# A 2048-step FFT convolution inside a GLU block: 28-channel spectrum steps, no exchanged filter loads, half of the second inverse turn through HBM

## The chip, the core and the metric

The kernel runs on one core of one Trainium2 chip. The metric is the device time of one execution in microseconds (us). Engines are named as in the profile: PE (matrix multiplier; PEld is its weight load), DVE (vector engine), ACT (scalar engine), POOL (GpSimd), SP (the queue that issues nearly all DMAs).

## The reference, cut to what matters

```python
x = A_q                                              # [1, 2048, 448], S = 2048, D = 448
sa, ca, ga, sb, cb, gb = split6(silu(c) @ w_mod)     # six rows of 448
h = layernorm(x) * (1 + ca) + sa
kv = causal_conv4(A_k, shift_k) * A_v                # four taps per channel
y = irfft(rfft(kv, 4096) * rfft(ssm_k, 4096))[:2048] + kv * ssm_D   # per channel
x = x + ga * (h * y)
h = layernorm(x) * (1 + cb) + sb
x = x + gb * ((sigmoid(h @ w_gate) * (h @ w_up)) @ w_down)          # 448 -> 1792 -> 448
```

## The kernel before

All of it is float32; the last part splits its operands in two fp32r pieces and multiplies three times.

**Convolution.** The long convolution is a product of spectra. A spectrum is made in three moves. Stage 1 is a matmul (`stage1_k` for the filter, `stage1_v` for the signal). Then `turn(a, i)` swaps, with one DVE instruction, the 32 partitions of each block with the 32 rows, for 28 channels: eight turns (`i` = 0 to 7) do the 224 channels of one half `h` of the model's 448. Stage 2 is a second matmul. The signal's two halves lie in `av[0]` and `av[1]`, the filter's in `ak[0]` and `ak[1]`; each is a tile of 128 partitions x 32 rows x 224 channels. The filter's second half takes its turn through HBM (`turn_out`, `turn_in`, tile `kd`), so `stage2_k(1, n)` can run only when those loads have landed.

**The loop `stage2_v`.** It has 16 steps, p = 8h + n. Step p takes a block of one eighth of `av[h]` (`block`): eight of the 32 rows and 112 of the 224 channels, so the first four blocks need turns 0 to 3 and the last four need turns 4 to 7. A step is: matmuls `s2v` into PSUM, two DVE products `m` with the filter's block (L306 for h = 0, L304 for h = 1), and, one step later, `stage2_back`: matmuls `sa` (L319) and an ACT copy back into `av[h]` (L320). For h = 0 the `s2v` matmuls are made twice, the second time with the real and imaginary rows exchanged. For h = 1 they are made once, and instead the filter's block is loaded once more with its partition groups exchanged: `load_kx`, four DMAs for each step into `kx`.

After every step `beside(h, n)` runs what is placed beside that step by a table on p: further turns, `stage2_k(1, .)`, the sums of the modulation (`mod_load`, `mod_parts`, `mod_sum`), the first layer norm (`ln1_stats` on ACT, `ln1_end` on DVE), and `gates`, which prepares the gate tiles `G` (on POOL; a part on ACT for the second half).

**The inverse.** The spectra take a turn back before the last matmul `stage_out` (tiles `y`). For `av[0]`, channels 0 to 111 go through HBM (`half_out`, `half_in`, scratch `kd0`) and channels 112 to 223 take four DVE turns. For `av[1]` all eight turns are DVE's: p = 13, 14, 15 and five after the loop. `gate` multiplies `y` by `G` and adds to `x1`: on POOL for h = 0, on DVE for h = 1.

**The tail and the GLU.** Between loop and GLU stand the last modulation sums, the first weights' split in two pieces (`split_hi` on ACT, `split_lo` on DVE, L501), `gate(1, 0)`, the second norm (`ln2_stats`, `ln2_end`), `norm_rows` and its transposes (`xn`, `pt`, L732). Then come 56 blocks of gate-and-up matmuls (`gu`, L760) and the down matmuls (`d`, L783), until the end.

Instructions stand in the order of the code (`tc.manual_schedule()`); each engine takes its own in that order and waits on semaphores. The PSUM tiles are `t` (two buffers), `sa` and `y` (one each).

Of the kernel before, what the change touches and what calls it, by code (L numbers as in the profile page):

```python
# [79 lines left out]
def adaln_conv_glu_kernel(ctx: ExitStack, tc: tile.TileContext, q, kT, v, ssm, shift, dskip,  # L80
# [201 lines left out]
    cols4 = lambda t: t.rearrange("p b (j c) -> p b j c", c=DT)  # L282

    def stage2_v(between):


        for h in range(2):
            for n in range(8):
                x, k = block(av[h], n), block(ak[h], n)
                if h:  # L290
                    kx = kxs.pop(n)
                    pt = two("t", f"s2v{h}_{n}")
                    stage2(pt, x)
                else:
                    pts = [two("t", f"s2v{h}_{n}_{b}") for b in range(2)]
                    for ex in range(2):
                        for b in range(2):
                            for r in (0, 64):
                                c = r ^ 64 * b
                                PE.matmul(pts[b][c:c + 64, ex, :D], w2[r:r + 64, ex], x[r:r + 64, b], start=True, stop=True)  # L300
                m = [pairs(quad("m", 4, f"m{h}_{n}_{b}")) for b in range(2)]
                for b in range(2):
                    if h:
                        DVE.tensor_mul(cols4(m[b]), cols4(rows(pt)), kx if b else k)  # L304
                    else:
                        DVE.tensor_mul(cols4(m[b]), cols4(rows(pts[b])), k[:, b].unsqueeze(1).to_broadcast([P, 2, 4, DT]))  # L306
# [4 lines left out]
        stage2_back()

    def stage2_back():
        h, n, m = products.pop(0)
        pt = two("sa", f"sa{h}_{n}")
        for b in range(2):
            for ex in range(2):
                r = slice(64 * ex, 64 * ex + 64)
                PE.matmul(pt[r, b, :D], wa[:, b, r], m[ex][:, b] if h else m[b][:, ex], start=True, stop=True)  # L319
        ACT.activation(block(av[h], n), cols4(rows(pt)), AF.Copy)  # L320

    kxs = {}

    def load_kx(n):

        kx = quad("kx", 2, f"kx{n}").rearrange("p a c -> p (a c)").rearrange("p (b j c) -> p b j c", b=2, c=DT)
        x = block(ak[1], n)
        for r in range(0, P, 32):
            nc.sync.dma_start(kx[r:r + 32], x[r ^ 32:(r ^ 32) + 32])
        kxs[n] = kx  # L330
# [314 lines left out]
    raw = lambda i: late["tmp"][:, NG * C + 512 * i:NG * C + 512 * (i + 1)]

    def beside(h, n):

# [15 lines left out]
        if p in (4, 5) or 8 <= p < 14:  # L664
            load_kx(p - 4 if p < 6 else p - 6)
        if 7 <= p < 11:
            half_in(av[0], kd0, half, p - 7)
        if p in (2, 5, 8, 9):
            ln1_end({2: 0, 5: 1, 8: 2, 9: 3}[p])
        if p in (2, 5) or 8 <= p < 14:  # L670
            next(gating)
        if p in (0, 1, 3, 4, 6, 7):
            ln1_stats({0: 2, 1: 3, 3: 4, 4: 5, 6: 6, 7: 7}[p])
# [2 lines left out]
        if p in (9, 10):
            turn(av[0], 2 * p - 14)
            turn(av[0], 2 * p - 13)
        if p >= 13:
            turn(av[1], p - 13)  # L680
        if p in (12, 13):
            for k in range(3):
                load_raw(0, 3 * (p - 12) + k, raw(3 * (p - 12) + k))
        if p >= 13:
            gate(0, p - 13, y_copy(0, p - 13, stage_out(0, p - 13, "y")), POOL)
# [6 lines left out]
    gate(0, 3, y_copy(0, 3, stage_out(0, 3, "y")), POOL)
    for m in (3, 5):
        mod_parts(m, "sa")
        mod_sum(m)
    rb_.close()
# [232 lines left out]
```

## Time and profile before

| | |
|---|---|
| median of 3 runs | 617.83 us (617.62 to 618.08) |
| the profiled execution's own time | 617.9 us |
| its span, first to last instruction | 616.1 us |
| PE busy | 573.5 us (93% of the span) |
| DVE, ACT, POOL busy | 330.6, 245.3, 80.2 us |
| mean granted PE clock | 0.982 |

A busy share of the whole span says little here: up to about 225 us the work is spread over all engines, after it PE runs almost without a gap. Times below are in us from the span's start.

### The profile page before, as it was taken

The page shows a single profiled execution, that of the slowest core. Times are in us where ns is not written, and L with a number is a line of the kernel's source. Part 1 is how long each engine was busy: PE and PEld are TensorE (multiplying, and loading weights), DVE is VectorE, ACT ScalarE, POOL GpSimd, SP SyncE. Part 2 cuts the span into 40 slices and gives each one's busy share as a digit, 9 for nine tenths or more (in the row PEclk, how much of TensorE's full clock was granted, in tenths as well). Part 3 has the DMA queues.
Part 4 walks back from the last instruction along what each step waited for, and adds up shares of the span by engine and source line. Part 5 has one row for each costly group of instructions (what it writes and reads, how often), then busy time and mean ns, then how long its engine had stood idle before and what let it go on. Part 6 is the DMA issues. An engine that isn't in the chain of part 4 may idle for free.

```text
span 616.1 us, 7497 instructions
## 1 busy us (share of the span) xinstructions
PE 573.5 (93%) x3020; PEld 435.5 (71%) x3020; DVE 330.6 (54%) x409; ACT 245.3 (40%) x429; POOL 80.2 (13%) x69
## 2 busy tenths in 40 slices
PE   7997598979769999999999999999999999999995
PEld 6554222324357788888888888888888888888884
DVE  0999888897987874433443333333334434433332
ACT  5998675776346675511222221222122112211110
POOL 2000004499930000000100000000010001000000
PEclk9999989999879999999999999999999999999999
DMA  8996899688521100000111110111011101000112
GB/s 295 273 324 243 265 214 287 148 163 188 139 66 50 35 1 1 0 1 0 31 51 33 35 41 10 30 35 34 1 30 35 36 0 31 0 1 26 65 60 90
DMA packets 36919, 51.88 MB, mean 84 GB/s; under 512 B 18834, under 2 KB 25748, under 8 KB 36756
## 3 DMA queue, kind: packets, MB, share of 16 engines
q1 hardware_dynamic: 36820, 51.39, 30.2%
q8 instruction: 24, 0.39, 0.3%
q14 instruction: 11, 0.09, 0.0%
q0 software_dynamic: 64, 0.01, 0.0%
HBM read 38.55 MB, written 9.18 MB: 77 GB/s over the span
## 4 chain that ended last, share of the span: by engine, by line
PE 69%; DVE 12%; ACT 7%; DMA 6%; issue 3%; SPq 1%; DVEq 0%; ACTq 0%
PE gu L760 40%; PE d L783 20%; DVE av L175 3%; DMA v<-in_v_dram 2%; PE sa L319 2%; DMA wm<-in_wmod_dram 2%; PE s2v L300 1%; PE pt L732 1%; DMA kT<-in_kT_dram 1%; DVE acc L227 1%; DVE m L306 1%; DMA ssm<-in_ssm_dram 1%; ACT xn L720 1%; DVE st L417 1%; DVE x L786 1%
## 5 line engine op out<-in xcount | busy, mean ns | idle before, releaser
L760 PE MATMUL gu<-xt,wt 128*128 128x512 f32 x1232 | 291.0, 391 | 1.2 <-DVE sg L765 1.2
L760 PEld LDWEIGHTS gu<-xt,wt 128*128 128x128 f32 x1232 | 230.9, 188 | 47.9 <-DVE sg L765 1.7
L765 DVE TENSOR_TENSOR sg<-sg,gu 128x512 f32<-128x512 f32 x56 | 38.4, 686 | 185.4 <-ACT sg L764 185.2
L783 PE MATMUL d<-wt,hh 128*128 128x448 f32 x448 | 127.7, 366 | 3.0 <-DVE x L786 2.7
L764 ACT ACTIVATE sg<-gu 128x512 f32<-128x512 f32 x56 | 33.4, 597 | 236.5 <-PE gu L760 236.5
L783 PEld LDWEIGHTS d<-wt,hh 128*128 128x128 f32 x448 | 83.9, 188 | 13.2 <-issue 1.9
L783 PE MATMUL d<-wt,hl 128*128 128x448 f32 x224 | 81.8, 365 | 0.0
L786 DVE TENSOR_TENSOR x<-x,d 128x896 f32<-128x896 f32 (+1 forms) x57 | 60.7, 1066 | 5.6 <-PE d L783 5.6
L769 DVE TENSOR_TENSOR hl<-sg,hh 128x512 fp32r<-128x512 f32 x56 | 39.2, 700 | 39.2 <-ACT hh L768 39.2
L768 ACT ACTIVATE hh<-sg 128x512 fp32r<-128x512 f32 x56 | 35.4, 633 | 45.6 <-DVE sg L765 45.6
L486 POOL TENSOR_TENSOR r<-r,gbrow 128x448 f32<-128x448 f32 x10 | 11.5, 1157 | 313.4 <-DMA r<-in_wd_dram 307.3
L175 DVE STREAM_TRANSPOSE av<-av 128x896 f32<-128x896 f32 x28 | 50.2, 1841 | 0.0
L783 PEld LDWEIGHTS d<-wt,hl 128*128 128x128 f32 x224 | 42.1, 188 | 3.3
L319 PE MATMUL sa<-m,wa 128*64 128x448 f32 x128 | 30.3, 552 | 5.4 <-DVE m L304 2.1
L319 PEld LDWEIGHTS sa<-m,wa 128*64 128x64 f32 x128 | 8.4, 136 | 26.0 <-issue 14.3
L300 PE MATMUL s2v<-av,w 64*64 64x448 f32 x128 | 17.6, 599 | 5.8 <-DVE av L175 5.6
L320 ACT ACTIVATE av<-sa 128x896 f32<-128x896 f32 x16 | 14.6, 913 | 18.8 <-PE sa L319 18.8
L455 POOL TENSOR_SCALAR G<-x,rstd,nmr 128x224 f32<-128x224 f32 x16 | 8.3, 530 | 96.3 <-DMA wm<-in_wmod_dram 83.5
L306 DVE TENSOR_TENSOR m<-s2v,ak 128x896 f32<-128x896 f32 x16 | 16.6, 1079 | 5.8 <-PE s2v L300 5.7
L501 DVE TENSOR_TENSOR wt<-r,wt 128x512 fp32r<-128x512 f32 (+1 forms) x30 | 19.7, 663 | 0.0
L175 DVE STREAM_TRANSPOSE ak<-ak 128x896 f32<-128x896 f32 x8 | 13.9, 1825 | 8.8 <-ACT ak L199 8.8
L495 ACT ACTIVATE wt<-r 128x512 fp32r<-128x512 f32 (+1 forms) x30 | 17.7, 597 | 0.0
(112 smaller groups left out, 515.8 us busy)
## 6 DMA issues: line engine op xcount, KB each, us to landing
wm<-in_wmod_dram SPq DMA_DIRECT2D x10, 392.0 KB, 5.2
kd<-ak SPq DMA_DIRECT2D x4, 896.0 KB, 8.4
x<-in_q_dram SPq DMA_DIRECT2D x4, 896.0 KB, 11.8
ak<-kd SPq DMA_DIRECT2D x4, 896.0 KB, 15.8
kx<-ak SPq DMA_DIRECT2D x32, 112.0 KB, 3.8
out_dram<-x SPq DMA_DIRECT2D x7, 448.0 KB, 2.5
v<-in_v_dram SPq DMA_DIRECT2D x6, 448.0 KB, 9.8
r<-in_wg_dram SPq DMA_DIRECT2D x10, 256.0 KB, 2.7
```

The lines of the kernel that those rows point to most:

```text
L175: DVE.transpose(x, x)
L300: PE.matmul(pts[b][c:c + 64, ex, :D], w2[r:r + 64, ex], x[r:r + 64, b], start=True, stop=True)
L306: DVE.tensor_mul(cols4(m[b]), cols4(rows(pts[b])), k[:, b].unsqueeze(1).to_broadcast([P, 2, 4, DT]))
L319: PE.matmul(pt[r, b, :D], wa[:, b, r], m[ex][:, b] if h else m[b][:, ex], start=True, stop=True)
L501: DVE.tensor_sub(lo, r, hi)
L760: PE.matmul(pgu[:, s], wts[j][s][k % 2][:, t, f * P:(f + 1) * P], x[:, xs], start=first, stop=not left)
L764: ACT.activation(sg, pgu[:, 0], AF.Sigmoid)
L765: DVE.tensor_mul(sg, sg, pgu[:, 1])
L768: ACT.activation(hh, sg, AF.Copy)
L769: DVE.tensor_sub(hl, sg, hh)
L783: PE.matmul(pt[:, i, :D], h[:, (2 * e + i) * P:(2 * e + i + 1) * P], w[:, f], start=m == 0, stop=m == len(ops) - 1)
L786: DVE.tensor_add(y, y, rows(pt)[:, a:b])
```

## The change

**Blocks.** For h = 0, and for the last four blocks of h = 1, a block is now all 32 rows of the 28 channels of one turn. The first four blocks of h = 1 (`eights`) keep eight rows, and the first 112 channels. Both halves now make the `s2v` matmuls twice, so `load_kx` and its 32 DMAs are gone.

**Stage 1.** The last four groups of `stage1_v` (12 to 15) become `stage1_v_half`: two groups at a time, `av[0]` first, `av[1]` after it, copied by ACT alone; `mod_parts(0)` stands between.

**Turns.** Two turns stand ahead of the loop where there were five; a table `TURNS` places the others. Channels 0 to 111 of `av[1]` come back through HBM: `eight_out` after steps 9 to 12, `half_in` after step 13. Four inverse turns of `av[1]` remain, the last one after the loop.

**Beside the steps and in the tail.** `gates` takes another order, and its eight steps stand after steps 3, 4 (two), 5, 7, 9, 10 and 11 (before: 2, 5 and 8 to 13); the modulation sum for the scale of `cols` goes from step 5 to step 12; `stage_out` of h = 0 comes one step sooner (p = 12 to 15); the first raw weights load after steps 9 to 11; the last modulation parts stand between the `y1` matmuls; `ln2_stats` and `ln2_end` of the first rows follow the first `gate` directly; `gate(1, 1)` stands ahead of `norm_split`.

The diff, cut:

```diff
+    def stage1_v_half(h, g):
+        pt = two("t", f"s1v{g}_{h}")
+        for j in range(2):
+            x = xin["v", g // 2][:, j, h * C:h * C + C]
...
+        ACT.activation(d[:, :, g * C:(g + 2) * C], rows(pt), AF.Copy)
...
+    def block(t, h, n):
+        x = t[:, n % 4 * 8:n % 4 * 8 + 8, :DT] if eights(h, n) else t[:, :, 28 * n:28 * n + 28]
...
-                if h:
-                    kx = kxs.pop(n)
-                    pt = two("t", f"s2v{h}_{n}")
-                    stage2(pt, x)
...
+    def eight_out(a, scratch, n, c):
+        nc.sync.dma_start(scratch[:, 8 * n:8 * n + 8, c], a[:, 8 * n:8 * n + 8, c])
...
-        for h, i in [(h, i) for h in range(2) for i in range(4)]:
+        for h, i in ((0, 0), (0, 1), (1, 0), (1, 1), (0, 2), (0, 3), (1, 2), (1, 3)):
...
-    s1v(*range(12, 16))
+    for h in range(2):
+        for g in (12, 14):
+            stage1_v_half(h, g)
+        if not h:
+            mod_parts(0, "sa", gbrow)
...
-    for n in range(5):
+    for n in range(2):
         turn(av[0], n)
...
+    TURNS = {0: ((0, 2),), 1: ((0, 3), (1, 0)), 2: ((0, 4), (1, 1)), 3: ((0, 5),), 4: ((0, 6), (1, 2)), 5: ((0, 7),), 6: ((1, 3),),
+             7: ((1, 4),), 8: ((1, 5),), 9: ((0, 4), (0, 5)), 10: ((0, 6), (0, 7)), 11: ((1, 6),), 12: ((1, 7),), 13: ((1, 4),),
+             14: ((1, 5),), 15: ((1, 6),)}
...
+        if 4 <= p < 12:
+            stage2_k(1, p - 4)
...
+        if p == 8:
+            half_in(av[0], kd0, half, *range(4))
+        if 9 <= p < 13:
+            eight_out(av[1], kd1, p - 9, half)
...
+        if p == 13:
+            half_in(av[1], kd1, half, *range(4))
+        if p in (3, 4, 7, 9):
+            ln1_end({3: 0, 4: 1, 7: 2, 9: 3}[p])
+        for _ in range({3: 1, 4: 2, 5: 1, 7: 1, 9: 1, 10: 1, 11: 1}.get(p, 0)):
+            next(gating)
+        if p in (0, 1, 2, 3, 5, 6, 7, 8):
+            ln1_stats(p if p < 4 else p - 1)
+        if p >= 12:
+            gate(0, p - 12, y_copy(0, p - 12, stage_out(0, p - 12, "y")), POOL)
...
-    for i in range(3, 8):
-        turn(av[1], i)
+    turn(av[1], 7)
...
+    mod_parts(5, "sa")
+    y1 = [stage_out(1, 0, "t")]
+    mod_sum(5)
+    for k in (4, 5):
+        gate_raw(0, k)
+    for k in range(4):
+        split_lo(0, k)
+    gate(1, 0, y1[0], DVE)
+    y1.append(stage_out(1, 1, "t"))
+    ln2_stats(0, 1, 2, 3, act=(0,))
+    mod_parts(3, "sa")
+    y1.append(stage_out(1, 2, "y"))
+    ln2_end(0, 1)
+    mod_sum(3)
+    y1.append(stage_out(1, 3, "sa"))
```

Names of one tile end in the tile's number; `av0`, `m0_1_0` and so on are the tile's name before it.

DVE where the loop begins, before (the last stage 1 copy, then turns, then the products of steps 0 and 1):

```order
L211 COPY av1_406<-s1v15_646 128x2x224
L175 STREAM_TRANSPOSE av0_405<-av0_405 128x28x32 x5
L306 TENSOR_TENSOR m0_0_0_713<-s2v0_0_0_703,ak0_153 128x896
L306 TENSOR_TENSOR m0_0_1_714<-s2v0_0_1_704,ak0_153 128x896
L175 STREAM_TRANSPOSE av0_405<-av0_405 128x28x32
L175 STREAM_TRANSPOSE av1_406<-av1_406 128x28x32
L306 TENSOR_TENSOR m0_1_0_744<-s2v0_1_0_734,ak0_153 128x896
```

The same place now:

```order
L175 STREAM_TRANSPOSE av0_405<-av0_405 128x28x32 x2
L312 TENSOR_TENSOR m0_0_0_703<-s2v0_0_0_693,ak0_153 128x896
L312 TENSOR_TENSOR m0_0_1_704<-s2v0_0_1_694,ak0_153 128x896
L175 STREAM_TRANSPOSE av0_405<-av0_405 128x28x32
L312 TENSOR_TENSOR m0_1_0_735<-s2v0_1_0_725,ak0_153 128x896
L312 TENSOR_TENSOR m0_1_1_736<-s2v0_1_1_726,ak0_153 128x896
L175 STREAM_TRANSPOSE av0_405<-av0_405 128x28x32
L175 STREAM_TRANSPOSE av1_406<-av1_406 128x28x32
```

Three turns of `av0` moved from ahead of the first product to behind it, and one turn of `av1` went from step 0 to a later step.

DVE at the loop's end, before (products of steps 14 and 15, the inverse turns of `av1`, the weights' low pieces, the first gate):

```order
L304 TENSOR_TENSOR m1_6_1_1217<-s2v1_6_1211,kx6_1153 128x896
L175 STREAM_TRANSPOSE av1_406<-av1_406 128x28x32
L304 TENSOR_TENSOR m1_7_0_1244<-s2v1_7_1239,ak1_154 128x896
L304 TENSOR_TENSOR m1_7_1_1245<-s2v1_7_1239,kx7_1183 128x896
L175 STREAM_TRANSPOSE av1_406<-av1_406 128x28x32 x6
L501 TENSOR_TENSOR wt0_1329<-tmp_1072,wt0_1329 128x512 x3
L360 TENSOR_TENSOR G1_0_1102<-G1_0_1102,y1_0_1343 128x896
```

The same place now:

```order
L312 TENSOR_TENSOR m1_6_1_1240<-s2v1_6_1_1230,ak1_154 128x896
L175 STREAM_TRANSPOSE av1_406<-av1_406 128x28x32
L312 TENSOR_TENSOR m1_7_0_1272<-s2v1_7_0_1262,ak1_154 128x896
L312 TENSOR_TENSOR m1_7_1_1273<-s2v1_7_1_1263,ak1_154 128x896
L175 STREAM_TRANSPOSE av1_406<-av1_406 128x28x32 x2
L501 TENSOR_TENSOR wt0_1306<-tmp_1049,wt0_1306 128x512 x4
L359 TENSOR_TENSOR G1_0_867<-G1_0_867,y1_0_1322 128x896
```

Four of the six turns behind the last products are gone, a fourth low piece stands there, and no product reads a `kx` tile.

PE between the loop and the GLU, before (`mod3`, `mod5` are modulation sums, `y1_i` the last inverse matmuls, `pt` the transposes):

```order
L384 MATMUL mod5_1315<-wm50_1277,scb_88 32x224 x4
L384 MATMUL mod5_1315<-wm51_1279,scb_88 32x224 x4
L393 MATMUL mod5_1315<-part5_1324,ones_82 128x448
L347 MATMUL y1_0_1343<-av1_406,wb_91 64x224 x8
L347 MATMUL y1_1_1352<-av1_406,wb_91 64x224 x8
L347 MATMUL y1_2_1361<-av1_406,wb_91 64x224 x8
L347 MATMUL y1_3_1370<-av1_406,wb_91 64x224 x8
L732 MATMUL pt0_0_1417<-ident_81,xn0_1411 128x128 x8
```

The same place now:

```order
L383 MATMUL mod5_1311<-wm51_1178,scb_88 32x224 x4
L346 MATMUL y1_0_1322<-av1_406,wb_91 64x224 x8
L393 MATMUL mod5_1311<-part5_1320,ones_82 128x448
L346 MATMUL y1_1_1341<-av1_406,wb_91 64x224 x8
L383 MATMUL mod3_1362<-wm30_1301,scb_88 32x224 x4
L383 MATMUL mod3_1362<-wm31_1303,scb_88 32x224 x4
L346 MATMUL y1_2_1373<-av1_406,wb_91 64x224 x8
L403 MATMUL mod3_1362<-ones_82,part3_1371 128x1 x3
L405 MATMUL mod3_1362<-ones_82,part3_1371 64x1 x2
L346 MATMUL y1_3_1392<-av1_406,wb_91 64x224 x8
L736 MATMUL pt0_0_1425<-ident_81,xn0_1419 128x128 x8
```

The modulation matmuls that stood ahead of the first `y1` now stand between the `y1` matmuls.

More of the change, by code (lines that the diff above doesn't have):

```diff
@@ L213, in stage1_v @@
                 ACT.activation(a, y, AF.Copy)
+    def stage1_v_half(h, g):
+        pt = two("t", f"s1v{g}_{h}")
+        for j in range(2):
+            x = xin["v", g // 2][:, j, h * C:h * C + C]
+            for s in range(2):
+                r = slice(64 * s, 64 * s + 64)
+                PE.matmul(pt[:, s, j * C:j * C + C], zc[r, g + j], x[r], start=True, stop=True)
+        d = av[h].rearrange("p (s j) c -> p s (j c)", s=2)
+        ACT.activation(d[:, :, g * C:(g + 2) * C], rows(pt), AF.Copy)
     acc = {}
@@ L288, in stage2_v @@
             for n in range(8):
-                x, k = block(av[h], n), block(ak[h], n)
-                if h:
-                    kx = kxs.pop(n)
-                    pt = two("t", f"s2v{h}_{n}")
-                    stage2(pt, x)
[L294 to L300, printed above, removed]
+                x, k = block(av[h], h, n), block(ak[h], h, n)
+                pts = [two("t", f"s2v{h}_{n}_{b}") for b in range(2)]
+                for ex in range(2):
+                    for b in range(2):
+                        for r in (0, 64):
+                            c = r ^ 64 * b
+                            PE.matmul(pts[b][c:c + 64, ex, :D], w2[r:r + 64, ex], x[r:r + 64, b], start=True, stop=True)
                 m = [pairs(quad("m", 4, f"m{h}_{n}_{b}")) for b in range(2)]
+                w = DT if eights(h, n) else 28
                 for b in range(2):
[L303 to L306, printed above, removed]
+                    DVE.tensor_mul(cols4(m[b], h, n), cols4(rows(pts[b]), h, n), k[:, b].unsqueeze(1).to_broadcast([P, 2, D // w, w]))
                 products.append((h, n, m))
@@ L318, in stage2_back @@
                 r = slice(64 * ex, 64 * ex + 64)
[L319 to L330, printed above, removed]
+                PE.matmul(pt[r, b, :D], wa[:, b, r], m[b][:, ex], start=True, stop=True)
+        ACT.activation(block(av[h], h, n), cols4(rows(pt), h, n), AF.Copy)
     def half_out(a, scratch, c):
         nc.sync.dma_start(scratch[:, :, c], a[:, :, c])
+    def eight_out(a, scratch, n, c):
+        nc.sync.dma_start(scratch[:, 8 * n:8 * n + 8, c], a[:, 8 * n:8 * n + 8, c])
     def half_in(a, scratch, c, *bs):
@@ L384, in mod_parts @@
                 PE.matmul(pr[32 * ct:32 * ct + 32, 0, h * C:(h + 1) * C], scb[:, ct], wm[:, ct], start=True, stop=True)
-        part = late["rb"].tile([P, D], F32, tag="part", bufs=1, name=f"part{m}")
+        if part is None:
+            part = late["rb"].tile([P, D], F32, tag="part", bufs=1, name=f"part{m}")
         ACT.activation(part, pr[:, 0, :D], AF.Copy)
@@ L663, in beside @@
             half_out(av[0], kd0, half)
[L664 to L673, printed above, removed]
+        if p == 8:
+            half_in(av[0], kd0, half, *range(4))
         if p == 9:
             late["tmp"] = big.tile([P, 32 * C], F32, tag="k0", name="tmp")
[L676 to L685, printed above, removed]
+        if 9 <= p < 13:
+            eight_out(av[1], kd1, p - 9, half)
+        if 9 <= p < 12:
+            for k in range(2 * p - 18, 2 * p - 16):
+                load_raw(0, k, raw(k))
+        if p == 12:
+            mod_load(5)
+        if p == 13:
[8 more added lines that the diff above has]
+            gate(0, p - 12, y_copy(0, p - 12, stage_out(0, p - 12, "y")), POOL)
     stage2_v(beside)
     mod_load(3)
-    mod_load(5)
-    for i in range(3, 8):
-        turn(av[1], i)
[L692 to L696, printed above, removed]
+    turn(av[1], 7)
     new_w(0)
@@ L798, in adaln_conv_glu_kernel @@
     norm_rows(0)
-    norm_turn(0, 0, "sa")
+    norm_turn(0, 0, "t")
     norm_turn(0, 2, "y")
+    gate(1, 1, yc[0], DVE)
     norm_split(0, 0)
     norm_split(0, 2)
-    gate(1, 1, yc[0], DVE)
     ln2_stats(4, 5, 6, 7, act=(4,))
```

53 lines of the change are left out of this document (20 added, 33 removed).

## The prediction

> **What bounds the kernel now.** I read the chain of waits first, then busy time and granted clock by stretch, then the groups of instructions, then the timeline from 60 to 200 us. The chain, by engine:
>
> ```profile
> PE 69%; DVE 12%; ACT 7%; DMA 6%; issue 3%; SPq 1%; DVEq 0%; ACTq 0%
> ```
>
> The busy time of each engine (with its count of instructions) in two stretches of 15 us, then PE clock, DMA share and GB/s:
>
> ```profile
> 90.00:105.00 15.00, 12.85 (x74) 3.43 (x70) 14.97 (x15) 8.90 (x20) 6.28 (x6) 1.00 1.06 283
> 210.00:225.00 15.00, 15.00 (x74) 12.95 (x73) 12.45 (x26) 9.84 (x21) 0.00 (x0) 1.00 0.07 19
> ```
>
> From about 210 us PE is full, and the change adds and takes nothing there: whatever the GLU's start gains, the end gains. So the sum is one date, the first `gu` matmul. Ahead of it DVE is the fullest engine (third figure, 14.97 of 15 us at 90). Groups, with the count, busy time and the mean of one in ns:
>
> ```profile
> L175 DVE STREAM_TRANSPOSE av<-av 128x896 f32<-128x896 f32 x28 | 50.2, 1841 | 0.0
> L306 DVE TENSOR_TENSOR m<-s2v,ak 128x896 f32<-128x896 f32 x16 | 16.6, 1079 | 5.8 <-PE s2v L300 5.7
> L320 ACT ACTIVATE av<-sa 128x896 f32<-128x896 f32 x16 | 14.6, 913 | 18.8 <-PE sa L319 18.8
> L501 DVE TENSOR_TENSOR wt<-r,wt 128x512 fp32r<-128x512 f32 x20 | 13.5, 685 | 0.0
> L361 POOL TENSOR_TENSOR x<-x,G 128x896 f32<-128x896 f32 x4 | 8.7, 2180 | 0.3
> ```
>
> **Ahead of the loop.** The timeline (start, duration):
>
> ```profile
> 64.53 1.77 PE L207 MATMUL s1v<-v,zc 64*128 64x448 f32 x8 [0.62 <-DVE av L211]
> 68.50 1.38 DVE L211 COPY av<-s1v 128x448 f32<-128x448 f32 x2 [0.95 <-ACT av L213]
> 69.80 8.55 DVE L175 STREAM_TRANSPOSE av<-av 128x896 f32<-128x896 f32 x5
> 76.81 3.27 PE L300 MATMUL s2v<-av,w 64*64 64x448 f32 x16 [5.55 <-DVE av L175]
> 80.11 2.09 DVE L306 TENSOR_TENSOR m<-s2v,ak 128x896 f32<-128x896 f32 x2 [1.75 <-PE s2v L300]
> ```
>
> Now: the two half matmul groups of `av[0]` are one 1.77 us, 64.53 to 66.3; their ACT copies, two of 0.91 us as L320, end at about 67.4. DVE's last four copies (two rows of 1.38 us, one of them shown) are gone, so the first turn starts at 67.4 instead of 69.80. The first modulation part (1 us) and the `av[1]` half (1.77) follow on PE until 69.1, and the last ACT copy frees the second `t` buffer at about 70.1. The first `s2v` needs one turn, not four, and both buffers: 70.1 plus some 1.4 us for what is left of it, so the first product starts at **71.5, not 80.11**. Three turns (8.55 for five, so 5.1 us) are thereby put off into the loop.
>
> **The loop.** Rows for the pace of a step:
>
> ```profile
> 85.58 2.03 DVE L306 TENSOR_TENSOR m<-s2v,ak 128x896 f32<-128x896 f32 x2
> 91.05 2.03 DVE L306 TENSOR_TENSOR m<-s2v,ak 128x896 f32<-128x896 f32 x2
> 111.73 1.68 PE L300 MATMUL s2v<-av,w 64*64 64x448 f32 x16
> 115.80 1.68 PE L300 MATMUL s2v<-av,w 64*64 64x448 f32 x16
> 144.90 0.98 PE L266 MATMUL s2v<-av,w 64*64 64x448 f32 x8
> 148.98 0.98 PE L266 MATMUL s2v<-av,w 64*64 64x448 f32 x8
> 71.74 0.57 ACT L432 ACTIVATE gbrow<-x 128x448 f32<-128x448 f32 x1
> 74.73 0.58 ACT L432 ACTIVATE gbrow<-x 128x448 f32<-128x448 f32 x1
> 96.50 0.57 DVE L395 TENSOR_TENSOR arow<-arow,mod 128x448 f32<-128x448 f32 x1
> 154.32 1.09 DVE L304 TENSOR_TENSOR m<-s2v,kx 128x896 f32<-128x896 f32 x1 [2.94 <-DMA kx<-ak]
> 155.33 10.54 DVE L175 STREAM_TRANSPOSE av<-av 128x896 f32<-128x896 f32 x6
> ```
>
> A step with two products and two turns takes 5.47 us (80.11, 85.58, 91.05); turns in a row are 1.76 apart, so one turn less is 3.7. A PE step with doubled `s2v`, `sa` and `s2k` takes 4.07 (111.73 to 115.80). One with single `s2v`, `sa` and `y` takes 4.08 (144.90 to 148.98); doubling adds 0.70 (1.68 against 0.98), so 4.8. That 0.70 is paid in all eight steps of h = 1, but shows only where PE is last. ACT's pair of statistics takes 2.99 (71.74 to 74.73), with `sa` and `s2k` copies of 0.91 each 4.8 a step; it starts ahead of DVE and I let it hide in steps 5 to 8.
>
> Step by step, whichever is last: 0: 3.8. 1 and 2: 5.5 each. 3: one turn, `arow` and `brow` (0.57 each) and the norm's two small ones (0.16 each, below): 5.1. 4: two turns, small ones, lock (below): 7.3. 5, 6, 8: PE, 4.1 each. 7: one turn, small ones, lock: 5.6. 9: 5.8. 10: 5.5. 11: 4.2. 12: PE with `s2v`, `sa`, `y` (4.8) and a modulation sum (1.1): 5.9. 13, 14: PE, 4.8 each. 15: `sa`, `y`, the last `sa` (5.0), its ACT copy (0.9), the last turn (1.8), hops: 7.9. Sum 84.0, so **the last turn ends at 155.5, not 165.87** (155.33 + 10.54): 10.4 us. The loop itself shrinks only from 85.8 to 84.0: the four inverse turns (7.0) and the `kx` waits (2.94 at 154.32, the longest) pay for the three turns moved in, PE's doubled matmuls and the locks. The rest of the 10.4 is the earlier start.
>
> The lock. One row is from the timeline, one from the view of the line L441 (shortest/median/longest in ns, first and last start):
>
> ```profile
> 125.95 2.09 POOL L456 TENSOR_TENSOR G<-G,arow 128x896 f32<-128x896 f32 x1
> L441 DVE TENSOR_TENSOR nmr<-nmr,rstd x4: 161/164/1657, 97.7 to 126.4; 128x4 f32<-128x4 f32 x4
> ```
>
> L441, four numbers wide, takes 0.16 us, but 1.66 at 126.4, until POOL's L456 ends at 128.04: a DVE operation with two SBUF inputs waits out a running POOL one. The gates come earlier now, and POOL works through steps 4 and 7; I charge 1.5 us in each. Bounds: 0, and a whole POOL operation, 2.1.
>
> **The tail.** From the last turn to the first `gu` is 17.5 us before (one row is a stretch of 3 us, with the granted clock third from its end):
>
> ```profile
> 166.78 6.26 DVE L501 TENSOR_TENSOR wt<-tmp,wt 128x512 fp32r<-128x512 f32 x3 [0.91 <-ACT wt L495]
> 172.96 1.07 DVE L360 TENSOR_TENSOR G<-G,y 128x896 f32<-128x896 f32 x1
> 175.27 0.63 DVE L417 BATCH_NORM_STATS2 st<-x 128x6 f32<-128x448 f32 x1
> 178.83 1.78 DVE L718 TENSOR_SCALAR xn<-x,rstd,nmr 128x448 f32<-128x448 f32 x4
> 179.54 4.15 PE L732 MATMUL pt<-ident,xn 128*128 128x128 f32 x16 [4.98 <-ACT tmp L353]
> 180.64 0.29 DVE L721 COPY xn<-xn 128x256 f32<-128x256 f32 x1
> 180.00:183.00 3.00, 3.00 (x13) 2.53 (x13) 1.06 (x4) 0.98 (x2) 1.14 (x1) 0.50 0.26 73
> 183.34 10.61 PE L760 MATMUL gu<-xt,wt 128*128 128x512 f32 x44
> 195.20 5.32 PE L760 MATMUL gu<-xt,wt 128*128 128x512 f32 x22 [1.25 <-DVE sg L765]
> ```
>
> Three low pieces took 6.26 us beside POOL's gates; 685 ns each is their price alone. Now there are four, while only POOL's last gate still runs (its four gates, each a multiply like L456's 2.09 and an add of 2.18, 17.1 in all, start with `y0` at about 137): 2.8 + 1.4 = 4.2. Gate 2.2 (172.96 to 175.2), statistics and norm 3.0 (175.27 to 178.3), `xn` and copy 2.1, then `gate(1, 1)`, 2.2 as the first, then the first cast 0.5: 14.2. **The first `gu` starts at 169.7, not 183.34: 13.6 us.** What moved on PE hides beside these 14.2: four `y1` (about 1.5 each: 4.08 less 0.98 for `s2v`, halved between `sa` and `y`), the modulation groups of `mod5` and `mod3`, some 4 together (an estimate: each moves about as many columns as half an `s2v` group or two), and `pt`, which took 4.15 at half clock (0.50) and about half of that at full: 12 in all. If that cover went, 1 to 3 us would come out.
>
> `gate(1, 1)` no longer stands in front of the second statistics and so of ACT's sigmoid, and the wait of 1.25 us at 195.20 goes. The sigmoid is then due about two us before the 10.61 us of the first two blocks are over; if that cover is gone, up to 1.25 comes back.
>
> The filter loads may be late for the new step 4, whose `s2k` comes at about 92. From the view of their tile, the landing times (shortest, median, longest) and the first and last issue, and from the timeline the first `s2k` of before:
>
> ```profile
> DMA to landing us min/median/max: 10.6/15.8/19.7
> L187 SPq DMA_DIRECT2D ak<-kd x4: 423/2486/4956, 69.5 to 75.1; - x4
> 97.65 1.08 PE L266 MATMUL s2k<-ak,w 64*64 64x448 f32 x8 [1.13 <-DVE brow L396]
> ```
>
> The last of the four is issued at 75.1, so 94.8 at the worst: between 0 and 2.8 late; I take 1.0, since the median lands in time. The other DMA edits cost nothing: 32 `kx` issues leave SP's queue. `half_in` of `av[0]` now waits there for its scratch to be written, with only `eight_out` and the first raw weights behind it, wanted 15 us later. Behind `half_in` of `av[1]` stand the loads of `mod_load(3)` and of the second weights; the tail wants these last.
>
> Sum against the profiled execution: 13.6 + 1.25 - 1.0 = 13.9, 617.9 - 13.9 = **604.0 us** (617.83, the median, stands within 0.1 of it). Its own range, by the lock and loading bounds and 3 us for the pacing: 600 to 607.5.
>
> **Rivals.** *A, the HBM way of `av[1]` ends late.* It leaves after the copy of `sa` in step 12, at about 135, and must be back for `y1` at 155.5. The rows of the same way of `av[0]`, KB of one and us to landing:
>
> ```profile
> kd<-av SPq DMA_DIRECT2D x1, 1792.0 KB, 11.1
> av<-kd SPq DMA_DIRECT2D x4, 448.0 KB, 5.2
> ```
>
> A last quarter of 2.8 and four loads one after another (20.8) land at 158.6: 607. With 11.1 for the quarter 167: 615.5. For it: SP waits in order. Against: the four loads can overlap, and DMA is idle there with `kx` gone. Chance 0.13.
>
> *B, the lock bites everywhere.* If POOL's gates run later than I have them, all four low pieces and the two gate operations wait: 1.4 x 3 more, 2 for the gates, and another 1.5 at step 9: 611.5. Chance 0.14. [...]
>
> *C, slower.* The products, copies and matmuls now step over runs of 28 floats. If a product cost what a turn costs, 1.84 for 1.08, the 24 on strips add 18.2: 622, past no change from 0.58 each. Against: L721 copies 256 elements in runs of 64 in 0.29, as cheap per element as long runs. Chance 0.06.
>
> *D, the change doesn't bring the early start:* the loads (DMA share 1.06 at 90 us) keep step 4 at its old date, 5.7 late: about 609. Chance 0.06.
>
> *E, more is won:* no lock, PE never at half clock: 599. Chance 0.08.
>
> The forecast has 0.51; 0.02 is left for no change. 598 to 611.5 leaves out A's upper end, C and the rest, 0.15 in all. Faster by over 0.2% (about what a measurement of this kernel tells from none; 1.2 us) 0.91, within it 0.02, slower 0.07 (C, and A with B).
>
> **What would show it.** First turn at 67.4, first product at 71.5, two-turn steps of 5.5, PE steps of 4.8 at the end, last turn at 155.5, first `gu` at 169.7, no wait on `sg` behind it. Products above 1.3 us would show C; a wait of `y1` on a DMA, A; L501 above 1 us more than once, B. I am wrong most simply if the waits that I let hide on ACT in steps 5 to 8 come out: up to 0.7 in each (4.8 against 4.1).

## The result and the profile after

The changed kernel takes **601.2 us** (median of four runs, 600.19 to 604.44), where the kernel before takes 617.86: a ratio of 0.9743, 95% interval 0.971 to 0.9777. It is faster. The forecast was 604.0 in a range of 598 to 611.5. Measured again on another chip it took 600.8 (600.02 to 601.25; 0.9718, 0.9705 to 0.9731).

The first profiled execution, 604.44, is the slowest of these; that of the second measurement, 600.62, lies by the medians. Both are needed here: what parts them is, for the most part, the one wait that the forecast mis-sized. First two lines of the first one's page: busy time by engine, and the shares of the chain that ended last.

```profile
PE 572.8 (95%) x3100; PEld 437.2 (73%) x3100; DVE 319.1 (53%) x401; ACT 245.5 (41%) x429; POOL 80.0 (13%) x69
...
PE 75%; DVE 8%; ACT 7%; DMA 5%; issue 2%; SPq 2%; DVEq 0%; ACTq 0%
```

PE's busy time is what it was (573.5), the span 13.4 us shorter: waiting time went. DVE's share of the chain fell from 12% to 8%. The dates that carry the sum stand in the timeline (start, duration, engine, line; in brackets the idle time ahead and what ended it). Second measurement:

```profile
67.29 3.56 DVE L175 STREAM_TRANSPOSE av<-av 128x896 f32<-128x896 f32 x2 [2.28 <-ACT av L224]
71.04 2.09 DVE L312 TENSOR_TENSOR m<-s2v,ak 128x896 f32<-128x896 f32 x2 [0.19 <-PE s2v L308]
...
93.25 3.62 DVE L175 STREAM_TRANSPOSE av<-av 128x896 f32<-128x896 f32 x2
93.84 0.60 PE L277 MATMUL s2k<-ak,w 64*64 64x448 f32 x3 [1.25 <-DMA ak<-kdk]
95.96 2.10 POOL L457 TENSOR_TENSOR G<-G,brow 128x896 f32<-128x896 f32 x1
96.95 1.13 DVE L441 TENSOR_TENSOR nmr<-nmr,rstd 128x4 f32<-128x4 f32 x1
98.00 2.08 DVE L312 TENSOR_TENSOR m<-s2v,ak 128x896 f32<-128x896 f32 x2
...
152.26 1.93 DVE L175 STREAM_TRANSPOSE av<-av 128x896 f32<-128x896 f32 x1 [1.15 <-ACT av L326]
154.09 3.33 DVE L501 TENSOR_TENSOR wt<-tmp,wt 128x512 fp32r<-128x512 f32 x4
154.25 3.26 PE L346 MATMUL y<-av,wb 128*64 128x224 f32 x16 [1.00 <-DVE av L175]
168.39 15.28 PE L764 MATMUL gu<-xt,wt 128*128 128x512 f32 x66 [0.77 <-DVE xt L746]
```

The same stretch in the first execution:

```profile
67.81 3.61 DVE L175 STREAM_TRANSPOSE av<-av 128x896 f32<-128x896 f32 x2 [2.28 <-ACT av L224]
71.58 2.09 DVE L312 TENSOR_TENSOR m<-s2v,ak 128x896 f32<-128x896 f32 x2 [0.16 <-PE s2v L308]
...
96.00 1.02 PE L277 MATMUL s2k<-ak,w 64*64 64x448 f32 x3 [3.05 <-DMA ak<-kdk]
96.82 3.93 PE L308 MATMUL s2v<-av,w 64*64 64x448 f32 x15
100.75 2.09 DVE L312 TENSOR_TENSOR m<-s2v,ak 128x896 f32<-128x896 f32 x2 [2.37 <-PE s2v L308]
110.49 1.73 PE L325 MATMUL sa<-m,wa 128*64 128x448 f32 x8 [0.98 <-ACT av L326]
...
172.29 15.27 PE L764 MATMUL gu<-xt,wt 128*128 128x512 f32 x66 [1.00 <-DVE xt L746]
```

Up to step 4 the two agree within 0.6 us. There PE waited 3.05 us for the filter loads, not 1.25, and then ran its `s2v` matmuls in 3.93, not 2.03 us (94.28 in the second). The stretches of 2 us in the first execution show why (the number ahead of the DMA share, third from the end, is PE's granted clock):

```profile
92.00:94.00 2.00, 0.95 (x4) 0.17 (x2) 2.00 (x3) 0.92 (x1) 2.00 (x4) 1.00 1.11 302
94.00:96.00 2.00, 0.00 (x0) 0.03 (x1) 2.00 (x2) 0.00 (x0) 1.92 (x2) 0.79 1.04 337
96.00:98.00 2.00, 2.00 (x12) 0.85 (x16) 1.97 (x3) 0.19 (x1) 1.92 (x2) 0.50 1.02 237
...
100.00:102.00 2.00, 2.00 (x8) 0.53 (x6) 1.25 (x2) 0.58 (x2) 1.92 (x3) 0.51 0.98 318
```

PE stood still up to 96.00, and when it went on it had half its clock (0.50), until 102: the wait was paid nearly twice.

All dates in one table (us; a step's length is the time from its first product to that of the next):

| | before | forecast | again (600.62) | first (604.44) |
|---|---|---|---|---|
| first turn | 69.80 | 67.4 | 67.29 | 67.81 |
| first product | 80.11 | 71.5 | 71.04 | 71.58 |
| step 4 | | 7.3 | 6.75 | 9.14 |
| steps 5 to 8 together | | 17.9 | 16.76 | 18.71 |
| last turn ends | 165.87 | 155.5 | 154.19 | 158.82 |
| first `gu` | 183.34 | 169.7 | 168.39 | 172.29 |
| from there to the end | 432.8 | 431.5 | 430.4 | 430.4 |

### The profile page after: what moved, and what is told of

The parts are those of the page before. It is cut to its first block, busy times and chain, and to the rows that moved or that the text cites. A ratio compares the mean times of both kernels' runs of the same rounds, so it can differ in the third digit from the quotient of the medians.

```text
span 602.7 us, 7614 instructions
## 1 busy us (share of the span) xinstructions
PE 572.8 (95%) x3100; PEld 437.2 (73%) x3100; DVE 319.1 (53%) x401; ACT 245.5 (41%) x429; POOL 80.0 (13%) x69
## 4 chain that ended last, share of the span: by engine, by line
PE 75%; DVE 8%; ACT 7%; DMA 5%; issue 2%; SPq 2%; DVEq 0%; ACTq 0%
PE gu L764 44%; PE d L787 21%; DMA ak<-kdk 3%; PE sa L325 2%; DVE acc L238 2%; PE s2v L308 2%; SPq L187 1%; PE s2k L277 1%; PE s1k L198 1%; ACT ak L199 1%; DMA ssm<-in_ssm_dram 1%; ACT gbrow L433 1%; PE pt L736 1%; ACT ak L283 1%; ACT gbrow L432 1%
## 5 line engine op out<-in xcount | busy, mean ns | idle before, releaser
L175 DVE STREAM_TRANSPOSE av<-av 128x896 f32<-128x896 f32 x24 | 44.5, 1881 | 4.9 <-ACT av L326 2.7
L312 DVE TENSOR_TENSOR m<-s2v,ak 128x896 f32<-128x896 f32 x32 | 33.4, 1088 | 8.0 <-PE s2v L308 5.4
L308 PE MATMUL s2v<-av,w 64*64 64x448 f32 x256 | 33.2, 571 | 0.6 <-DVE av L175 0.5
L325 PE MATMUL sa<-m,wa 128*64 128x448 f32 x128 | 28.2, 562 | 2.6 <-ACT av L326 2.6
L308 PEld LDWEIGHTS s2v<-av,w 64*64 64x64 f32 x256 | 10.6, 138 | 17.5 <-issue 12.0
L277 PE MATMUL s2k<-ak,w 64*64 64x448 f32 x128 | 16.9, 578 | 3.7 <-DMA ak<-kdk 3.0
L501 DVE TENSOR_TENSOR wt<-r,wt 128x512 fp32r<-128x512 f32 (+1 forms) x30 | 19.7, 662 | 0.0
```

The lines of the kernel that those rows point to most:

```text
L175: DVE.transpose(x, x)
L277: PE.matmul(pt[c:c + 64, b, :D], w2[r:r + 64, 0], x[r:r + 64, b], start=True, stop=True)
L312: DVE.tensor_mul(cols4(m[b], h, n), cols4(rows(pts[b]), h, n), k[:, b].unsqueeze(1).to_broadcast([P, 2, D // w, w]))
L325: PE.matmul(pt[r, b, :D], wa[:, b, r], m[b][:, ex], start=True, stop=True)
```

## The experiments

Each kernel is the changed one with the edit shown; times are medians of four to six runs beside runs of the kernel before, and are set against 600.8 to 601.2. The kernel before, run beside each, took 617.6 to 618.1, so the chips differ little. Dates from their traces are set against the second measurement.

**The changed kernel once more.**

> The changed kernel unaltered, beside the three that follow, so that effects of one to three us can be read on one chip. Every theory: 601.2, between 600.2 and 604.4.

600.8. It is the reference for what follows.

**The inverse turns of `av[1]` back on DVE.**

```diff
-        if 9 <= p < 13:
-            eight_out(av[1], kd1, p - 9, half)
...
-        if p == 13:
-            half_in(av[1], kd1, half, *range(4))
...
-    turn(av[1], 7)
+    for i in range(3, 8):
+        turn(av[1], i)
```

> The first four inverse turns of av[1] go back from HBM to DVE: three stand beside steps 13 to 15 as the later ones did, five behind the last products. Theory (DVE's row in the tail is the end's chain, and the HBM way is hidden): the last turn ends 4 x 1.85 = 7.4 us later and nothing else moves, 601.2 + 7.4 = 608.6. Rival 1 (the HBM way, 1.8 MB more, holds up other loads or SP's queue): what it costs comes back, so less than 6 us more, below 607. Rival 2 (PE's y1 and modulation groups are the tail's bound, about 12 us, and hide part of the turns): 3 to 5 us more, 604 to 606.

607.41 (0.9828, 0.9813 to 0.9843): about 6.4 more, between theory and rival 1.

```profile
148.50 2.09 DVE L312 TENSOR_TENSOR m<-s2v,ak 128x896 f32<-128x896 f32 x2 [0.92 <-PE s2v L308]
150.51 10.39 DVE L175 STREAM_TRANSPOSE av<-av 128x896 f32<-128x896 f32 x6
160.80 2.44 DVE L501 TENSOR_TENSOR wt<-tmp,wt 128x512 fp32r<-128x512 f32 x4
164.32 1.09 DVE L359 TENSOR_TENSOR G<-G,y 128x896 f32<-128x896 f32 x1 [1.08 <-PE y L346]
```

From the last products to the end of the last turn it is 12.40 us, not 7.57: 4.8 of the 7.4, since DVE now turns without a gap where it waited 0.53 and 1.15 us for the last copies and their PE work. Another 1.0 lies behind it: from the last turn to `gu` 15.17 us, not 14.20. There the gate waits 1.08 for `y1`: PE had stood idle for 5.83 us beside the turns, and its first `y1` took 3.25 us, where it takes 1.74 at a granted clock of 1.00 (first execution, 158.88). The profiled run, 608.24, lost 1.9 more ahead of it, in steps 5 and 7, behind a load wait of 1.55. So the theory's 7.4 is too much because the turns fill waits that DVE had anyway. Rival 1's bound of 607 is passed narrowly, and no trace shows its reason: `y1` of the changed kernel waits for DVE's last turn, not for a DMA.

**The tail in its old order.**

```diff
+    for m in (3, 5):
+        mod_parts(m, "sa")
+        mod_sum(m)
     new_w(0)
     for k in range(4):
         split_hi(0, k)
...
+    y1 = [stage_out(1, i, tag) for i, tag in enumerate(("sa", "t", "t", "y"))]
...
     norm_split(0, 2)
+    gate(1, 1, yc[0], DVE)
```

> Only the code behind the last turn takes the order of before: both modulation groups ahead of all y1, the four y1 in a row, low pieces and statistics behind them, gate(1, 1) behind norm_split. Theory (PE work was laid under DVE's chain and gate(1, 1) out of the sigmoid's way): from the last turn to the first gu 13.5 becomes 17.5 as before, and up to 1.25 on sg comes back: 605.2 to 606.4. Rival (DVE does the same operations in both orders and bounds the tail): 0 to 1 us more, 601 to 602.

611.77 (0.9901, 0.9888 to 0.9915): 10.8 more, twice the theory.

```profile
154.66 0.58 PE L383 MATMUL mod<-wm,scb 112*32 112x224 f32 x8 [1.02 <-ACT av L326]
161.17 1.86 PE L393 MATMUL mod<-part,ones 128*128 128x448 f32 x2 [0.72 <-ACT part L386]
163.07 0.54 ACT L398 ACTIVATE gbrow<-mod 128x448 f32<-128x448 f32 x1 [1.95 <-PE mod L393]
163.51 2.18 ACT L495 ACTIVATE wt<-tmp 128x512 fp32r<-128x512 f32 x4
164.16 3.36 DVE L501 TENSOR_TENSOR wt<-tmp,wt 128x512 fp32r<-128x512 f32 x3 [7.66 <-ACT wt L495]
177.83 11.49 PE L758 MATMUL gu<-xt,wt 128*128 128x512 f32 x44
```

Read the fence from below: DVE's first low piece waits for ACT's high piece, that one stands behind `gbrow`, this behind the modulation sums on PE, which could only begin when the last copy freed their PSUM tile. DVE is idle for 7.66 us, and PE's clock is half from 157 to 167 us (the 16 matmuls of `mod5` take 1.72 us there, 0.96 in the second measurement; the run's mean granted clock is 0.980, against 0.996). In the kernel before, turns stood there. So I read the tail's order as what makes the HBM way a gain; the old order together with the turns on DVE was not run. My theory took the old 17.5 us over as a sum of operations; it was a sum under cover, and the cover had gone (21.3 now). Another 2.5 us are lost behind the first `gu`, and the profiled run, 612.51, lost 2.2 in the steps ahead, behind a load wait of 2.34.

**Five turns ahead of the loop again.**

```diff
-    for n in range(2):
+    for n in range(5):
         turn(av[0], n)
...
-    TURNS = {0: ((0, 2),), 1: ((0, 3), (1, 0)), 2: ((0, 4), (1, 1)), 3: ((0, 5),), 4: ((0, 6), (1, 2)), 5: ((0, 7),), ...
+    TURNS = {0: ((0, 5),), 1: ((0, 6), (1, 0)), 2: ((0, 7), (1, 1)), 4: ((1, 2),), ...
```

> Five turns stand ahead of the loop again, the other DVE turns keep their order. The first product comes 5.6 us later (77.2 for 71.6); steps 3 and 5 lose their turn and step 4 one of two. Theory (the early start counts in full, and the steps that lose a turn are bound by PE or ACT at about 4 to 4.5): 5.6 less 0.6, 1.3 and 0.2 is 3.5 more, 604.7. Rival 1 (the filter loads land at 94 to 99 in any case, and step 4 at about 97 waits for nothing, where it waits now): 1 to 2 more, 602 to 603. Rival 2 (only DVE's total counts, the place of the turns does not): 0, 601.

603.56 (0.977, 0.9754 to 0.9787): 2.6 more; theory and rival 1 both in part. The first product comes 5.1 later (76.15). Step 3 gives back 1.6 (3.40) and step 4 2.1 (4.62: a turn and half a us of lock less), more than I took; but step 7 takes 1.6 more (6.68):

```profile
103.73 2.09 DVE L312 TENSOR_TENSOR m<-s2v,ak 128x896 f32<-128x896 f32 x2 [1.98 <-PE s2v L308]
112.72 0.18 DVE L440 RECIPROCAL rstd<-rstd 128x4 f32<-128x4 f32 x1 [0.98 <-ACT rstd L436]
112.93 1.63 DVE L441 TENSOR_TENSOR nmr<-nmr,rstd 128x4 f32<-128x4 f32 x1
```

The shorter steps only run up to ACT: its statistics end 0.98 us too late for DVE, and L441 then meets a POOL gate. So about half of the 5.1 us of early start is worth something.

**The price of the doubled `s2v`.**

```diff
-                pts = [two("t", f"s2v{h}_{n}_{b}") for b in range(2)]
+                pts = [two("t", f"s2v{h}_{n}_{b}") for b in range(1 if h else 2)]
+                if h:
+                    stage2(pts[0], x)
+                    pts *= 2
```

> For h = 1 the s2v matmuls are made once, and both products read the same PSUM tile (the exchanged rows are left out, so the spectra of h = 1 are other numbers): the price of giving up the exchanged filter loads. Theory (steps 11 to 15 are bound by PE, which has 1.66 of s2v, 1.66 of sa and 1.6 of y): 0.83 less in each of five steps, 4 us, 597. Rival (the chain from product over sa, copy and turn, or ACT, is the bound in these steps): 0 to 1 less, 600 to 601.

599.05 (0.9693, 0.968 to 0.9707): 1.9 less, half the theory. The steps do what it says:

```profile
136.19 0.98 PE L277 MATMUL s2v<-av,w 64*64 64x448 f32 x8
137.10 1.72 PE L329 MATMUL sa<-m,wa 128*64 128x448 f32 x8
138.65 1.68 PE L350 MATMUL y<-av,wb 128*64 128x224 f32 x16
```

Steps 11 to 15 together are 3.6 us shorter in this trace. But its steps 4, 5 and 7 are 2.2 longer than in the second measurement, behind a load wait of 2.49. What the median would be with equal waits is not measured, nor what the 32 filter loads cost that the doubling replaces.

**The filter loads issued earlier.**

```diff
     mod_load(0)
+    turn_in(ak[1], kd, range(4))
...
-    turn_in(ak[1], kd, range(4))
```

> The four loads that bring the filter's second half back are issued some 12 us earlier, behind the load of the first modulation weights, ahead of those of the second (the queues move 90 GB/s between 56 and 62, and over 200 from 68 on). Theory (PE's wait of 1.6 to 3.1 on these loads at about 92, and the half clock of 0.50 that follows it, are real losses on the chain): 2 to 4 less than the changed kernel, 597 to 599, and less spread. Rival 1 (DVE's two turns of that step, or ACT behind it, take over): 0 to 1 less. Rival 2 (the loads now hold up the modulation weights, the rows of x or wa for the first steps): 1 to 5 more.

610.37 (0.9864, 0.9844 to 0.9884): 9.6 more, rival 2, and worse than I had it. SP's queue and those who wait:

```profile
56.47 7.77 SPq L187 DMA_DIRECT2D ak<-kdk  x4
64.34 4.59 SPq L372 DMA_DIRECT2D wb<-in_wmod_dram  x2
80.04 0.97 PE L383 MATMUL mod<-wb,scb 112*32 112x224 f32 x8 [7.36 <-DMA wb<-in_wmod_dram]
85.70 2.09 DVE L312 TENSOR_TENSOR m<-s2v,ak 128x896 f32<-128x896 f32 x2 [10.71 <-PE s2v L308]
```

3.6 MB ahead of the second modulation weights make these 7.4 us late, PE's `s2v` stands behind them in order, and step 0 is 14.49 us instead of 4.07. All else is as before, and that tells something: step 4, now without any load wait, still takes 6.74 us.

**The need moved behind the landing.**

```diff
-        if 4 <= p < 12:
-            stage2_k(1, p - 4)
+        if 5 <= p < 13:
+            stage2_k(1, p - 5)
```

> stage2_k(1, n) stands beside step n + 5, not n + 4; the loads stay where they are. Theory (the same wait as in the run before, met from the other side: the need moves 5 us behind the landing): 2 to 4 less than the changed kernel, 597 to 599, less what an eighth s2k costs in step 12, which PE bounds (0.8): 598 to 600. Rival (ACT, with its statistics in steps 5 to 8, is the bound from there on, so that only the start of a queue moves): 0, 601.

602.84 (0.9753, 0.974 to 0.9767): 1.8 more; my theory falls. No load wait, and step 4 is 6.73. Step 12 pays 1.95 (8.31), because `y` stands behind a copy by ACT:

```profile
135.96 1.74 PE L346 MATMUL y<-av,wb 128*64 128x224 f32 x16 [1.04 <-ACT ak L283]
139.44 2.09 DVE L312 TENSOR_TENSOR m<-s2v,ak 128x896 f32<-128x896 f32 x2 [4.42 <-ACT tmp L352]
```

**The modulation for `cols` two steps earlier, and one.**

```diff
-        for m in {0: (0,), 1: (1,), 3: (2,), 12: (4,)}.get(p, ()):
+        for m in {0: (0,), 1: (1,), 3: (2,), 10: (4,)}.get(p, ()):
...
-        if p in (0, 2, 11):
-            mod_parts({0: 1, 2: 2, 11: 4}[p], "y")
+        if p in (0, 2, 9):
+            mod_parts({0: 1, 2: 2, 9: 4}[p], "y")
```

In the second run 11 and 10 stand for 10 and 9.

> The modulation matmuls for the scale of cols go from steps 11 and 12 to steps 9 and 10, which have two turns and are bound by DVE at about 5.5. Theory (steps 11 and 12 are bound by PE, with 1.04 of idle behind the s2k copy, 0.8 of parts, 1.3 of sums and 0.3 of idle on them): 2 less than the changed kernel, 599. Rival 1 (PE's wait on ACT only moves to steps 9 and 10, which have no slack left): 0 to 1 less. Rival 2 (in step 12 POOL's gate or DVE's product waits next): 0.

> The modulation matmuls for the scale of cols go from steps 11 and 12 to steps 10 and 11, one step and not two as in the run before. Theory (step 10 has two turns and slack on PE, and ACT has by then worked off its statistics, for which PE waited 3 us in step 9): step 12 shrinks from 6.36 to 4.9, step 11 grows by 0.3: 1.2 less than the changed kernel, 599.5. Rival (PE waits again on the s2k copy, and the parts come out in full in step 10): 0 to 1 more.

603.05 (0.9752, 0.9731 to 0.9773) and 600.73 (0.9714, 0.9697 to 0.9731). Two steps earlier: steps 11 and 12 shrink by 0.69 and 1.47, but step 9 grows from 5.78 to 8.34. PE, waiting for ACT, in that run:

```profile
118.59 0.98 PE L277 MATMUL s2k<-ak,w 64*64 64x448 f32 x8
122.54 0.96 PE L383 MATMUL mod<-wm,scb 112*32 112x224 f32 x16 [2.97 <-ACT ak L283]
```

ACT still had 3.2 us of statistics in front of the copy that frees the tile. The three steps together grow by 0.4 only; the rest of this trace's loss stands in steps 4, 5 and 7, behind a load wait of 2.19, and how much of the median's 2 us is due to the edit stays open. One step earlier it has worked them off: step 10 grows by 0.15 only, 12 shrinks by 1.47, but 11 grows by 0.75 and step 8 by 0.64. No difference that the runs can tell.

**The small multiplications on POOL.**

```diff
         DVE.reciprocal(r, r)
-        DVE.tensor_mul(m, m, r)
+        POOL.tensor_mul(m, m, r)
```

> The four small multiplications of the first norm (128x4, L441) are made by POOL, whose gates read them, in place of DVE, where two of them took 1.13 and 1.12 us beside a running gate and 0.16 without one. Theory (a DVE operation with two SBUF inputs waits out a running POOL operation, and DVE is the bound in steps 4, 7 and 9): 1.0 less in step 4 and in step 7, 0.2 in step 9: 2 less than the changed kernel, 598.6 to 599. Rival 1 (the filter loads in step 4, and ACT's statistics in step 7, end just behind it): 0 to 1 less, 600 to 601. Rival 2 (ACT's gates now wait for POOL's queue, which has 4.3 us for each gate): 1 to 2 more.

601.99 (598.98 to 603.14; 0.9725, 0.9699 to 0.9751): no verdict on the time, but the trace has one. The multiplication takes 0.20 us on POOL, and what was just behind it on DVE takes its place, as rival 1 said:

```profile
98.44 0.20 POOL L441 TENSOR_TENSOR nmr<-nmr,rstd 128x4 f32<-128x4 f32 x1
98.64 2.09 DVE L312 TENSOR_TENSOR m<-s2v,ak 128x896 f32<-128x896 f32 x2 [1.70 <-PE s2v L308]
112.14 0.18 DVE L440 RECIPROCAL rstd<-rstd 128x4 f32<-128x4 f32 x1 [1.00 <-ACT rstd L436]
```

**Stage 1 with DVE's copies.**

```diff
-    for h in range(2):
-        for g in (12, 14):
-            stage1_v_half(h, g)
+    s1v(*range(12, 16))
```

> The last four groups of stage 1 go group by group again, with DVE copying the second half; the rest stays. Theory (the first turn waits for DVE's copies, as before, 69.8 for 67.3, and every later date moves with it): 2 to 2.5 more than the changed kernel, 603. Rival (the steps up to 4 have slack, and the filter loads set step 4): 0 to 1 more, 601 to 602.

602.29 (0.975, 0.9729 to 0.9771): 1.3 more. The first turn is back at 69.53 and the first product 2.2 later, yet the last turn only 1.8. The rival is right in part, though not by its reason: step 4 takes 6.72 here, so the loads did not set it.

**Three edits together.** Two of the four filter loads issued behind the first modulation weights (`turn_in(ak[1], kd, range(2))`, the others where they stood), L441 on POOL, the modulation for `cols` beside steps 10 and 11.

> Three edits together, as a candidate: two of the filter's four loads are issued 12 us earlier (behind the first modulation weights, the other two where they stood), L441 goes to POOL, and the modulation matmuls for cols stand beside steps 10 and 11. Theory (step 4 is bound by DVE's wait for POOL when the loads land in time, and by the loads when they don't; with both out of the way two turns and two products are left): step 4 falls from 6.75 to 5.6, steps 11 and 12 from 11.0 to 10.3, the modulation weights lose nothing since only half the bytes stand ahead of them: 1.5 to 2 less than the changed kernel, 599, and no run above 600.5. Rival 1 (half the filter's bytes still make the second modulation weights late, as all of them did by 10 us): step 0 grows, 1 to 4 more, 602 to 605. Rival 2 (ACT's statistics in steps 5 to 8 take back what step 4 gives): 0 to 0.7 less, 600 to 601.

597.68, five of six runs between 597.17 and 599.18 and one at 604.53, of which there is no trace (0.9702, 0.9668 to 0.9735). The median is some 3.3 us below the changed kernel's, but with that one run the intervals overlap; whether it always wins stays open. The profiled run does what the theory says:

```profile
56.14 0.94 SPq L187 DMA_DIRECT2D ak<-kdk  x2
72.53 0.96 PE L383 MATMUL mod<-wb,scb 112*32 112x224 f32 x16
91.58 0.98 PE L277 MATMUL s2k<-ak,w 64*64 64x448 f32 x8
96.51 0.12 DVE L440 RECIPROCAL rstd<-rstd 128x4 f32<-128x4 f32 x1
96.57 2.05 DVE L312 TENSOR_TENSOR m<-s2v,ak 128x896 f32<-128x896 f32 x2
98.09 0.21 POOL L441 TENSOR_TENSOR nmr<-nmr,rstd 128x4 f32<-128x4 f32 x1
```

The weights are in time, `s2k` waits for nothing, DVE for neither PE nor POOL. Step 4 is 5.57 (6.75), step 7 4.07 (5.04), steps 11 and 12 10.27 (11.00); step 8 takes 0.7 back. Neither edit gave this alone: with the lock gone the loads, and the half clock after them, were the bound (7.29), with the loads in time the lock was (6.73).

**Step 4 in all traces**, PE's wait for the loads, the lowest granted clock in the 2 us stretches from 94 to 98, and the step:

| run | wait | clock | step 4 |
|---|---|---|---|
| first execution | 3.05 | 0.50 | 9.14 |
| doubling left out | 2.49 | 0.60 | 7.49 |
| old tail | 2.34 | 0.50 | 7.83 |
| `cols` two steps earlier | 2.19 | 0.52 | 7.35 |
| turns back on DVE | 1.55 | 0.50 | 6.84 |
| `cols` one step earlier | 2.18 | 1.00 | 6.72 |
| DVE's copies | 1.41 | 1.00 | 6.72 |
| second measurement | 1.25 | 1.00 | 6.75 |
| loads early; need late | 0 | 1.00 | 6.74; 6.73 |
| five turns ahead (one turn in step 4) | 0 | 1.00 | 4.62 |
| L441 on POOL | 2.04 | 0.50 | 7.29 |
| all three | 0 | 1.00 | 5.57 |

With the lock in place a wait of up to 2.2 us costs nothing at full clock: DVE's two products, two turns and the wait on POOL fill 6.73 us. What costs, by this table, is the half clock that follows the wait in some runs, and a longer wait.

## Why the prediction was right, and where it was off

| term (us gained) | forecast | second measurement | first execution |
|---|---|---|---|
| first turn sooner | 2.4 | 2.5 | 2.0 |
| first turn to first product | 6.2 | 6.6 | 6.5 |
| first product to last turn | 1.8 | 2.6 | -1.5 |
| tail to the first `gu` | 3.3 | 3.3 | 4.0 |
| behind it | 1.25 | 2.4 | 2.4 |
| filter loads | -1.0 | in the steps | in the steps |
| sum | 13.9 | 17.3 | 13.4 |

The median's gain is 16.7. That the first execution's 13.4 lies nearest the forecast is luck: 4.1 lost behind the loads, where 1.0 was charged, meet some 2.5 us that the other terms gained beyond the forecast. Undone one by one, HBM way, tail order, early loop and ACT's copies cost 6.4, 10.8, 2.6 and 1.3, which is more than the whole gain: they depend on each other.

**The start and the tail** came as worked out. The tail's 14.20 in the second measurement are the forecast's 14.2, though by luck in part: its first `y1` took 3.26 us, and without that it is 13.47, as in the first execution, where `y1` took 1.74 at a granted clock of 1.00.

**The steps.** Two-turn steps were 5.58, 5.53, 5.78 and 5.48 (forecast 5.5 to 5.8), PE's steps 13 and 14 4.77 and 4.83 (4.8). L441 took 1.13 and 1.12, some 0.97 above its 0.16 alone, where 1.5 was charged for the lock; steps 4 and 7 came 0.55 and 0.56 under the walk, more than the 0.8 by which the whole was too long. Steps 11 and 12, 0.44 and 0.46 longer than forecast, took part of it back.

**The failed step** is the charge of 1.0 us for late filter loads. The loads were late, by 1.25 to 3.05 us in every trace that left them and their `s2k` in place beside two turns. But the charge was added to a step that already held two turns and the lock; of waits beside each other only the last to end counts. By the table above it is 0 where the lock is in place and the clock stays full. Where it does come out it brings half a clock (0.50) with it and, as I feared for steps 5 to 8, ACT, for whose copies PE's `sa` waits (0.98 us at 110.49): 1.95 us there in the first execution. Then it is 4.1 us in all (87.24 for 83.15 from the first product to the last turn), beyond the bound of 2.8 that I gave. The trace in which it is 0 took 600.62, by the medians; of the other runs of this kernel only the first was traced, so how often it comes out stays open.

**Behind the first `gu`** the gain is 2.4, not 1.25. The wait on `sg` is gone, and the first 66 matmuls take 15.28 us where they took 10.61, 1.25 and 5.32; 0.66 of that lies in the matmuls, some of it in a better clock, which I had not charged (granted 0.50 from the first `gu` at 183.34 to about 184.0 before, 1.00 from 172 in the first execution). The last 0.5 I did not trace.

**The rivals.** A: `y1` waited for DVE alone. B: two locked L441 and about 0.9 in L501 (3.33 for four beside POOL, 2.44 in the run where POOL was done): the lock bites, not everywhere. C, by the first execution's groups:

```profile
L175 DVE STREAM_TRANSPOSE av<-av 128x896 f32<-128x896 f32 x24 | 44.5, 1881 | 4.9 <-ACT av L326 2.7
L312 DVE TENSOR_TENSOR m<-s2v,ak 128x896 f32<-128x896 f32 x32 | 33.4, 1088 | 8.0 <-PE s2v L308 5.4
```

1088 ns is the mean of 24 products over runs of 28 floats and eight over 112; it was 1079 before. In the second measurement a pair over runs of 28 took 2.09 us (at 71.04) and one over 112 took 2.08 (at 120.54): short runs cost these products nothing. D: step 4 began at 91.3, not at the old date. E named 599 for no lock and no half clock; the run with both out of the way, and a third edit in it, took 597.68.

## What to carry to other kernels

When two delays fall into one step, put a date on the end of each and count the later one; taking one away shows only the other, so edits that do nothing alone can be worth some us together. An order of instructions has a price only together with the work that covers it: the old tail cost 17.5 us under five turns and 21.3 without them. A load moved forward in a queue is paid by what it is moved ahead of (all four filter loads made step 0 14.49 us instead of 4.07; with two of them the modulation weights were in time); move the half that fits into the gap.
